# Ten more half modes of weights loaded singly, and the 64-row items moved into the middle of the output loop

## The chip, the cores and the metric

The kernel runs on one core of one Trainium2 chip. The metric is the device time of one execution in microseconds; lower is better. A core has a matrix engine (PE), three elementwise engines (DVE, ACT, POOL), a queue engine (SP), and 16 DMA engines that all queues share. DMAs are issued here from POOL (all weight loads, which also cast from float32 to float16), from SP (most stores) and from ACT.

## What is computed

Two stages, with inputs and output in float32:

```
attn = softmax(mask(q kT / 8)) v          q, k, v: 8 batches x 8 heads x 576 x 64
                                          heads 0-3: local mask; heads 4-7: strided mask
x    = attn, heads joined                 8 x 576 x 512
X    = rfft(x) over the 576 rows, first 64 modes
Y[m] = X[m] (w_r[m] + i w_i[m])           64 modes, each with two 512 x 512 matrices
u    = x + irfft(Y)
out  = u + relu(u w_ch)                   8 x 576 x 512
```

The weights w_r and w_i are 64 x 512 x 512 each, 134 MB in float32, and are read once.

## The kernel before, in words

**Order of the stages.** Attention runs first, batch by batch, while the first weights arrive. Its output is brought to the 64 modes by products with a table (`dft`). The modes are then multiplied in "half modes": the 512 input channels are split in two halves, and each pair (half, mode) has one 512 KB share of float16 weights per matrix half. `ORDER` lists all 128 half modes in the order in which they are loaded: 56 of half 1, 48 of half 0, then the last 8 of half 1 and the last 16 of half 0.

**Loading.** `w_fetch` loads two half modes at a time into one tile `wt` from the pool `pw`, which has five buffers (`NWBUF`). It is called after the second mode of a pair has been multiplied. A pair is loaded by two DMAs of 512 KB in SBUF, one from `moe_w_r` and one from `moe_w_i` (line 186), both on POOL's queue; each holds both modes of the pair. For the last four entries of `ORDER` (`i < 2 * NM - 4` is false) it uses four DMAs of 256 KB instead (line 190), in the order: first mode real, first mode imaginary, second mode real, second mode imaginary. Loads on POOL use eight completion semaphores in turn, so a load waits until the one eight before it has landed.

**The late modes.** `rest` holds the last 24 half modes. Between them PE also runs `renew`, which adds what is already known of the inverse transform to the kept rows: `v0s` (rows times `w_ch`) and `xos` (the rows themselves), and `v0h`, `xoh` for the last 64 rows of two batches. What remains after the last mode is the last quarter of the modes' spectra.

**The output loop.** After the last mode, `spec_z` and a transposition give the last spectra `zzs` (times `w_ch`) and `yys`. The output is then made in 18 items (lines 973 to 975). Each is 128 rows x 1024 columns in float32, 512 KB:

- items 0 to 7: two batches of the first four, one group of 128 rows each;
- items 8 to 15: one batch of the last four, two groups of rows;
- items 16 and 17: the last 64 rows (512 to 575) of four batches each.

Round `k` of the loop puts, on PE, the kept rows of item `k` into a PSUM pair (`v_early`), the kept rows of item `k-1` into another (`u_early`), and then the new part of both (`new_rows`, products with 32-row strips of the table `A3`, at line 1004 for the items with one batch and at 1013 for the others). ACT then takes Relu of item `k` (`v_done`), DVE adds item `k-1` into `osb` (`u_done`, line 1032), and SP stores it (line 1041). For the 64-row items, `u_done` makes four stores of 64 x 512 each (line 1044): two from SP and two from ACT. `osb` uses the five buffers of `pw`. PSUM holds three pairs "p" in turn and one pair "u": Relu parts and the even adds use "p", the odd adds "u".

**Two special places.** At `k == 6` (line 1080) a "p" pair is held for the second half of `spec_z`: four products, a copy by ACT into `zzs[1]`, and two copies by POOL into `zzs[2]` (`other`). Items of the last four batches need it. And `pieces` (line 1017) has item 0 taken in two halves by ACT, DVE and the stores, all others whole.

Of the kernel before, what the change touches and what calls it, by code (L numbers as in the profile page):

```python
# [19 lines left out]
NM = 64  # L20
# [36 lines left out]
def kernel(  # L57
# [10 lines left out]
    nc = tc.nc  # L68
# [17 lines left out]
    def psum(kind, half=False, pair=False):  # L86
        if pair:
            return pss[kind].tile([128, 2, 512], FP, tag=kind, name=kind)
        if half:
            return pss[kind].tile([128, 1024], F16, tag=kind, name=kind)  # L90
        return pss[kind].tile([128, 512], FP, tag=kind, name=kind)
# [65 lines left out]
    def w_fetch(n=1):  # L157
        for _ in range(n):
            i = len(w_tiles)
            if i >= 2 * NM:  # L160
                return
            half, m = ORDER[i]
            if i // 2 in GUEST:
                wt = big.tile([128, 2, 4, DM], F16, tag=GUEST[i // 2], name="wt")
            else:
                wt = pw.tile([128, 2, 4, DM], F16, tag="w", name="wt")
            single = []
            for ri, src in enumerate((moe_w_r, moe_w_i)):
                dst = wt[ds(64 * ri, 64)]
                rows = src[m : m + 2, ds(256 * half, 256), :].rearrange(  # L170
                    "m (p c) e -> p m (c e)", c=4
                )
                dst = dst.rearrange("p m c e -> p m (c e)")


                ones = range(2)
                if ri and not m:
                    ones = [1]
                elif i in UNEVEN and not ri:
                    a = 0  # L180
                    for n in UNEVEN[i]:
                        nc.gpsimd.dma_start(dst[a : a + n], rows[a : a + n])
                        a += n
                    continue
                elif i < 2 * NM - 4:
                    nc.gpsimd.dma_start(dst, rows)  # L186
                    continue
                single += [(j, ri, dst[:, j], rows[:, j]) for j in ones]
            for _, _, to, rows in sorted(single, key=lambda x: x[:2]):
                nc.gpsimd.dma_start(to, rows)  # L190
            w_tiles.extend((wt[:, 0], wt[:, 1]))
# [46 lines left out]
    def normalise(val, den, n, pieces, dst):  # L238
        rec = pin.tile([128, 8], FP, tag="rec", bufs=4, name="rec")
        nc.vector.reciprocal(out=rec[0:n, 0:pieces], in_=den)  # L240
        nc.vector.tensor_tensor(  # L241
            out=dst,
            in0=val.rearrange("p h (q c) -> p h c q", c=4),
            in1=rec[0:n, 0:pieces]
            .to_broadcast((n, pieces, 64))
            .rearrange("p h (q c) -> p h c q", c=4),
            op=AluOp.mult,
        )

    def act_copy(out, in_):  # L250
        nc.scalar.activation(out=out, in_=in_, func=ACTF.Copy)  # L251
# [333 lines left out]
    def mode_pair(slot, m):  # L585
        half = 1 - slot
        if m % 4 == 0:
            ypt[slot] = psum("y")
        yp = ypt[slot]
        steps = [(c, mm) for c in range(4) for mm in (m, m + 1)]  # L590
        if m == 0:
            steps.sort(key=lambda x: x[1])
        for c, mm in steps:
            wt = w_tiles[ORDER.index((half, mm))]
            pr = ds(0, 128 if mm else 64)
            a = 32 * (mm % 4)
            nc.tensor.matmul(  # L597
                yp[ds(a, 32), :],
                Xh[half][pr, c].rearrange("p b r (h m) -> p (b r h) m", h=2)[
                    :, :, mm % 32  # L600
                ],
                wt[pr, XC[c], :],
                start=(c == 0),
                stop=(c == 3),
                tile_position=(0, a),
            )
        if slot or m // 2 not in GUEST:
            w_fetch()
        if m % 4:
            yr = big.tile([128, DM], F16, tag="yr", name="yr")  # L610
            act_copy(yr, yp)
            queued.append(lambda: four_turned(slot, m - 2, yr))

    def mode(slot, m):
# [22 lines left out]
        if m % 2:  # L637
            w_fetch()
# [94 lines left out]
    def spec_z(g, bq, zp):  # L733
        for e in range(4):
            lhs = YS["YT"][:, e, g, ds(8 * bq, 8), :].rearrange("p x m -> p (x m)")
            nc.tensor.matmul(
                zp, lhs, w_chs["n"][:, e, :], start=(e == 0), stop=(e == 3)
            )
# [31 lines left out]
    strided_tokens()  # L770
    load_str(2, 2)
    w_fetch()

    def str_front(b):
# [192 lines left out]
    for n, i in enumerate([3, 5, 7] + list(range(8, 21))):  # L967
        b, t = n // 2, n % 2 * 2
# [3 lines left out]

    items = [((2 * P, 2 * P + 1), t) for t in range(4) for P in (0, 1)]
    items += [((b,), t) for b0 in (4, 6) for t in (0, 2) for b in (b0, b0 + 1)]
    items += [(range(b, b + 4), 4) for b in (0, 4)]
    LAST = len(items) - 1
    vps, ups, rls, osbs = {}, {}, {}, {}

# [6 lines left out]
    def other(spectra):  # L985
        for a in (0, 64):
            nc.gpsimd.tensor_copy(out=spectra[2][ds(64 - a, 64)], in_=spectra[1][ds(a, 64)])

    def v_early(k):
        vps[k] = psum("p", pair=True)  # L990
        for j, r in enumerate(own(items[k], v0s, v0h)):
            nc.tensor.matmul(vps[k][:, j], idn, r, start=True, stop=False)  # L992

    def u_early(k):
        ups[k] = psum(("p", "u")[k % 2], pair=True)
        for j, r in enumerate(own(items[k], xos, xoh)):
            nc.tensor.matmul(ups[k][:, j], idn, r, start=True, stop=False)

    def new_rows(k, acc, spectra):
        bs, t = items[k]  # L1000
        if len(bs) == 1:
            for j, src in ((0, spectra[1]), (1, spectra[2])):
                q = ds(32 * ((bs[0] + 2 * j) % 4), 32)
                nc.tensor.matmul(
                    acc[:, j], A3[q, out_cols(t + j)], src[q], start=False, stop=True
                )
            return
        for j, b in enumerate(bs):
            q = ds(32 * (b % 4), 32)
            o, cols = acc[:, j % 2], out_cols(t)  # L1010
            if t == 4:
                o = acc[ds(64 * (b % 2), 64), j // 2]
            nc.tensor.matmul(  # L1013
                o, A3[q, cols], spectra[b // 4][q], start=False, stop=True
            )

    def pieces(k):
        return [slice(0, 1), slice(1, 2)] if k == 0 else [slice(0, 2)]

    def v_done(k):  # L1020
        rl = ptr.tile([128, 2, 576], FP, tag=("xT", "rl")[k // 2 % 2], bufs=2, name="rl")
        rls[k] = rl[:, :, 0:DM]
        vp = vps.pop(k)
        for j in pieces(k):
            nc.scalar.activation(out=rls[k][:, j], in_=vp[:, j], func=ACTF.Relu)  # L1025

    def u_done(k):
        bs, t = items[k]
        up, rl = ups.pop(k), rls.pop(k)
        osb = pw.tile([128, 2, DM], FP, tag="w", name="osb")  # L1030
        for j in pieces(k):
            nc.vector.tensor_tensor(
                out=osb[:, j], in0=up[:, j], in1=rl[:, j], op=AluOp.add
            )
            if t < 4:
                rows = out[:, ds(128 * (t - t % 2), 256), :].rearrange(
                    "b (p i) e -> p b i e", i=2
                )
                own_b = slice(bs[0] + j.start, bs[0] + j.stop)
                to = rows[:, own_b, t % 2] if len(bs) > 1 else rows[:, bs[0], j]  # L1040
                nc.sync.dma_start(to, osb[:, j])
        if t == 4:
            for b in bs:
                (nc.scalar if b % 2 else nc.sync).dma_start(
                    out[b, ds(512, 64), :], osb[ds(64 * (b % 2), 64), b // 2 % 2, :]
                )

# [26 lines left out]
    for k in range(2):  # L1074
        if k:
            u_early(k)
        new_rows(k, ups[k], yys)
        u_done(k)
    for k in range(2, LAST + 2):
        if k == 6:  # L1080
            held = psum("p", pair=True)[:, 0]
            spec_z(3, 1, held)
            act_copy(zzs[1], held)
            other(zzs)
        if k <= LAST:
            v_early(k)
        if k > 2:
            u_early(k - 1)
        if k <= LAST:
            new_rows(k, vps[k], zzs)  # L1090
        if k > 2:
            new_rows(k - 1, ups[k - 1], yys)
        if k <= LAST:
            v_done(k)
        if k > 2:
            u_done(k - 1)
# [31 lines left out]
```

## Time and profile before

| | us |
|---|---|
| Median of 6 runs | 428.17 |
| Lowest and highest | 427.74, 429.11 |
| The profiled execution's own time | 429.11 |
| Its span in the profile | 427.3 |
| DMA busy share, average rate | 214 GB/s over the span |
| PE busy | 346.2 (81%) |
| DVE, ACT, POOL busy | 234.8, 218.2, 113.2 |
| Mean granted PE clock | 0.926 |

How to read it. The span is what the profile covers, from the first to the last instruction; the time of the execution holds a little more. Busy time of PE is modelled from pipelined matmuls, so a busy PE is not PE at its peak. The page cuts the span into 40 slices of 10.7 us and gives each engine's busy share in tenths. GB/s counts the bytes as they are written, so a float32 weight that arrives as float16 counts half. A chain of waits goes back from the last instruction to what released it, and so on; what stands in it set the end. "Landing" of a DMA is the time from its issue until all of its parts have reported.

### The profile page before, as it was taken

How to read it: one execution, taken by the hardware profiler on the slowest of the kernel's cores; microseconds unless marked ns; L12 is line 12 of the kernel's file. 1: busy time of each engine (PE TensorE's matmuls, PEld its weight loads, DVE VectorE, ACT ScalarE, POOL GpSimd, SP SyncE). 2: the span in 40 equal slices, each digit the busy share in tenths (PEclk: the TensorE clock that was granted, in tenths of full speed). 3: DMA queues.
4: the chain of work that ended last, by engine and by line, in shares of the span. 5: the costliest groups of instructions: out<-in, count | busy, mean ns of one | idle time of the engine just before them, and what ended most of it. 6: DMA issues, size and time to landing. Idle time of an engine off the chain costs nothing.

```text
span 427.3 us, 9773 instructions
## 1 busy us (share of the span) xinstructions
PE 346.2 (81%) x4167; PEld 207.4 (49%) x4167; DVE 234.8 (55%) x466; ACT 218.2 (51%) x390; POOL 113.2 (26%) x200
## 2 busy tenths in 40 slices
PE   2977878779998598789678788877879768998993
PEld 2866766654656355556433344434445323454330
DVE  3788778851446054356203247736675462564794
ACT  1687778642666356565542234422442543453772
POOL 8332333322423222222221322232232221310200
PEclk9999999957999899999985899989999985899999
DMA  8999999999999999999999999999999999995697
GB/s 152 207 212 213 212 214 212 211 211 211 214 215 212 213 212 215 214 214 213 212 214 210 212 214 215 210 212 215 212 208 214 214 213 214 214 212 100 246 372 268
DMA packets 29914, 91.62 MB, mean 214 GB/s; under 512 B 4464, under 2 KB 5232, under 8 KB 29872
## 3 DMA queue, kind: packets, MB, share of 16 engines
q0 software_dynamic: 25168, 81.28, 96.2%
q1 hardware_dynamic: 3952, 9.13, 5.7%
q8 instruction: 32, 0.52, 0.5%
q10 hardware_dynamic: 752, 0.61, 0.5%
q14 instruction: 10, 0.08, 0.0%
HBM read 162.83 MB, written 9.44 MB: 403 GB/s over the span
## 4 chain that ended last, share of the span: by engine, by line
DMA 54%; PE 24%; DVE 12%; ACT 4%; issue 2%; POOL 1%; DVEq 0%; ACTq 0%; POOLq 0%
DMA wt<-in_moe_w_i_dram 44%; DMA wt<-in_moe_w_r_dram 9%; PE y L597 5%; DVE xb L241 3%; DVE kz L283 3%; PE p L992 2%; ACT X L251 2%; PE sc L532 2%; DVE rec L240 1%; DMA ring<-in_q_dram 1%; PE tp L413 1%; PE sc L459 1%; PE y L532 1%; DVE kz L420 1%; PE av L392 1%
## 5 line engine op out<-in xcount | busy, mean ns | idle before, releaser
L597 PE MATMUL y<-wt,X 128*32 128x512 f16 (+1 forms) x448 | 69.5, 423 | 22.9 <-DMA wt<-in_moe_w_i_dram 22.9
L186 POOL DMA_DIRECT2D wt<-in_moe_w_r_dram x59 | 34.7, 588 | 115.7 <-PE y L597 24.1
L186 POOL DMA_DIRECT2D wt<-in_moe_w_i_dram x60 | 35.4, 589 | 79.0 <-DMA wt<-in_moe_w_i_dram 54.9
L597 PEld LDWEIGHTS <-X 128*32 128x32 f16 (+1 forms) x448 | 27.9, 140 | 41.1 <-DMA wt<-in_moe_w_i_dram 21.6
L727 DVE COPY xo<-tp 128x512 f16<-128x512 f16 x32 | 22.1, 691 | 36.6 <-PE tp L725 36.6
L726 ACT ACTIVATE v<-sc 128x512 f16<-128x512 f32 x32 | 19.1, 597 | 44.3 <-PE sc L717 44.3
L717 PE MATMUL sc<-w_cp,xT 128*128 128x512 f16 x128 | 36.9, 410 | 1.9 <-DVE xT L690 1.9
L241 DVE TENSOR_TENSOR xb<-av,rec 90x256 f16<-90x256 f32 (+2 forms) x80 | 36.0, 450 | 2.8
L251 ACT ACTIVATE yr<-y 128x512 f16<-128x512 f32 x28 | 16.7, 597 | 40.4 <-PE y L597 39.3
L489 ACT ACTIVATE PL<-sc 128x480 f16<-128x480 f32 (+1 forms) x48 | 26.9, 578 | 20.3 <-PE sc L475 19.9
L240 DVE RECIPROCAL rec<-av 90x4 f32<-90x4 f32 (+2 forms) x80 | 14.6, 183 | 38.6 <-PE av L504 29.2
L961 DVE TENSOR_TENSOR xo<-p,xo 128x1024 f16<-128x1024 f32 x16 | 19.6, 1224 | 21.2 <-PE p L760 21.2
L420 DVE COPY qT<-tp 128x576 f16<-128x576 f16 x16 | 11.9, 752 | 33.8 <-PE tp L413 33.8
L251 ACT ACTIVATE v<-p 128x1024 f16<-128x1024 f32 x16 | 16.4, 1024 | 20.7 <-PE p L760 20.7
L378 ACT ACTIVATE PL<-sc 90x360 f16<-90x360 f32 (+1 forms) x48 | 22.7, 490 | 6.9 <-PE sc L371 6.3
L251 ACT ACTIVATE v<-tp 128x640 f16<-128x640 f16 (+1 forms) x24 | 19.0, 807 | 11.6 <-PE tp L447 8.9
L413 PE MATMUL tp<-cI_s,ring 64*64 64x64 f16 x864 | 22.9, 198 | 2.1 <-DVE qT L420 1.7
L459 PE MATMUL sc<-cMl_s,cI_s 128*128 128x480 f16 (+1 forms) x48 | 18.7, 391 | 5.3 <-ACT PL L489 3.7
L276 PE MATMUL tp<-cI_s,ring 72*128 72x72 f16 x256 | 15.4, 207 | 8.6 <-DMA ring<-in_v_dram 7.2
L251 ACT ACTIVATE kz<-tp 64x360 f16<-64x360 f16 (+1 forms) x32 | 18.9, 592 | 6.2 <-PE tp L413 5.2
L413 PEld LDWEIGHTS <-ring 64*64 64x64 f16 x864 | 18.0, 112 | 8.3 <-issue 4.2
L1025 ACT ACTIVATE rl<-p 128x1024 f32<-128x1024 f32 (+1 forms) x19 | 18.4, 979 | 5.9 <-PE p L1013 2.0
(148 smaller groups left out, 742.0 us busy)
## 6 DMA issues: line engine op xcount, KB each, us to landing
wt<-in_moe_w_i_dram POOLq DMA_DIRECT2D x60, 512.0 KB, 18.8
wt<-in_moe_w_r_dram POOLq DMA_DIRECT2D x59, 512.0 KB, 18.0
out_dram<-osb SPq DMA_DIRECT2D x15, 512.0 KB, 2.8
ring<-in_v_dram POOLq DMA_DIRECT2D x8, 288.0 KB, 13.3
ring<-in_q_dram POOLq DMA_DIRECT2D x8, 288.0 KB, 13.6
ring<-in_k_dram POOLq DMA_DIRECT2D x8, 288.0 KB, 13.0
ring<-in_v_dram POOLq DMA_DIRECT2D x3, 512.0 KB, 14.5
ring<-in_q_dram POOLq DMA_DIRECT2D x3, 512.0 KB, 14.5
```

Of the source, the lines that this page charges most:

```text
L186: nc.gpsimd.dma_start(dst, rows)
L241: nc.vector.tensor_tensor(out=dst, in0=val.rearrange("p h (q c) -> p h c q", c=4), in1=rec[0:n, 0:pieces] .to_broadcast((n, pieces, 64)) . ...
L251: nc.scalar.activation(out=out, in_=in_, func=ACTF.Copy)
L378: nc.scalar.activation(out=PS[0:n, ds(POFF[t], 4 * n)], in_=scp[0:n, 0 : 4 * n], func=ACTF.Exp, scale=SCALE,)
L413: nc.tensor.transpose(tp[ds(64 * hp, 64), ds(64 * i, 64)], qn[ds(64 * hp, 64), ds(64 * (9 * g + i), 64)], idn[ds(64 * hp, 64), ds(64 * hp, ...
L459: nc.tensor.matmul(scp[:, 0 : n * times].rearrange("p (h x) -> p h x", h=times), idn, mask_rows("cMl", n, times), start=True, stop=False,)
L489: nc.scalar.activation(out=dst, in_=src, func=ACTF.Exp, scale=SCALE)
L597: nc.tensor.matmul(yp[ds(a, 32), :], Xh[half][pr, c].rearrange("p b r (h m) -> p (b r h) m", h=2)[:, :, mm % 32], wt[pr, XC[c], :], start= ...
L717: nc.tensor.matmul(vp, xT[:, ch], w_chs["cp"][:, ch, :], start=(ch == 0), stop=(ch == 3),)
L726: nc.scalar.activation(out=v0, in_=vp, func=ACTF.Copy)
L727: nc.vector.tensor_copy(out=xo.rearrange("p (h q c) -> p h q c", h=2, c=4), in_=tp[:, 0:512].rearrange("p (h c q) -> p h q c", h=2, c=4),)
L961: nc.vector.tensor_tensor(out=xo, in0=up[:, 0:n], in1=xo, op=AluOp.add)
```

## The change

1. `w_fetch` loads the last fourteen entries of `ORDER` singly instead of the last four: the five pairs of half modes before the last two pairs now come by twenty DMAs of 256 KB instead of ten of 512 KB. The order in which bytes are asked for changes inside each pair: first mode's real and imaginary parts, then the second mode's.
2. The two items of the last 64 rows move from the end of the list to places 8 and 13. The items of one batch are now 9 to 12 and 14 to 17.
3. The item that is last is now a whole item of 128 rows. It is taken in two halves, as item 0 is: two Relus, two adds, two stores of 256 KB.
4. Of the four stores of a 64-row item, the two that ACT issued are now issued by GpSimd (POOL).
5. The held product for `zzs[1]` moves from round 6 to round 7, since the item at place 8 doesn't read it.

```diff
@@ w_fetch
-                elif i < 2 * NM - 4:
+                elif i < 2 * NM - 14:
                     nc.gpsimd.dma_start(dst, rows)
                     continue
@@ the items
     items += [((b,), t) for b0 in (4, 6) for t in (0, 2) for b in (b0, b0 + 1)]
-    items += [(range(b, b + 4), 4) for b in (0, 4)]
+    items.insert(8, (range(0, 4), 4))
+    items.insert(13, (range(4, 8), 4))
     LAST = len(items) - 1
@@ pieces
-        return [slice(0, 1), slice(1, 2)] if k == 0 else [slice(0, 2)]
+        return [slice(0, 1), slice(1, 2)] if k in (0, LAST) else [slice(0, 2)]
@@ u_done
             for b in bs:
-                (nc.scalar if b % 2 else nc.sync).dma_start(
+                (nc.gpsimd if b % 2 else nc.sync).dma_start(
                     out[b, ds(512, 64), :], osb[ds(64 * (b % 2), 64), b // 2 % 2, :]
                 )
@@ the loop
     for k in range(2, LAST + 2):
-        if k == 6:
+        if k == 7:
             held = psum("p", pair=True)[:, 0]
             spec_z(3, 1, held)
```

On the engines' queues, PE, DVE and ACT keep their instructions in number and kind but for the halves: those of item 0's kind appear a second time at the end. POOL's queue gains ten weight loads and, behind its last copies, four stores. SP's queue has its four stores of 64 rows in the middle and two half stores at the end. ACT's queue ends with its last two Relus and no store.

## The prediction

> **What bounds the kernel now.** I read the page first (the engines' lines, the DMA line, the chain), then the chain in order of time for the last 65 us, then the timeline of the last 35 us, the stores' lines and the stretches of DMA share. From the page:
>
> ```profile
> span 427.3 us, 9773 instructions
> DMA  8999999999999999999999999999999999995697
> DMA 54%; PE 24%; DVE 12%; ACT 4%; issue 2%; POOL 1%; DVEq 0%; ACTq 0%; POOLq 0%
> ```
>
> The DMA engines are full until slice 36 (some 390 us); then comes another regime. The chain in order of time:
>
> ```profile
> 363.93 18.16 DMA wt<-in_moe_w_i_dram
> 382.09 0.28 issue
> 382.37 10.16 DMA wt<-in_moe_w_i_dram
> 392.54 0.14 issue
> 392.67 0.65 PE y L630 x16
> ...
> 401.95 1.01 ACT rl L1025
> 402.96 0.04 issue
> 403.01 0.59 PE p L992 x2
> ```
>
> The end is set by the last weights (landed at 392.54), then by a tail of 34.8 us. POOL's last weight load went out only when the load eight before it had landed (382.09): eight can be under way. In the tail the chain is PE with three visits elsewhere; one is the stall at 403.01, where PE waits for a Relu. The timeline at the tail's end:
>
> ```profile
> 417.14 0.41 PE L1013 MATMUL p<-zz,cFl_s 32*64 32x512 f16 x4
> 417.48 0.39 PE L1004 MATMUL u<-yy,cFl_s 32*128 32x512 f16 x2
> 417.80 0.60 PE L992 MATMUL p<-v0h,cI_s 128*128 128x512 f16 x2
> ...
> 420.64 1.22 DVE L1032 TENSOR_TENSOR osb<-u,rl 128x1024 f32<-128x1024 f32 x1
> 420.75 2.44 SPq L1044 DMA_DIRECT2D out_dram<-osb  x4
> 420.76 2.73 ACTq L1044 DMA_DIRECT2D out_dram<-osb  x4
> ```
>
> A normal round of the item loop starts 1.29-1.30 us after the one before (L992 at 408.39, 409.69, 410.99); the round with the first 64-row item takes 1.63 (416.17 to 417.80). DVE is done at 421.86, and 5.5 us follow in which only stores are left. Those stores, by their line:
>
> ```profile
> L1044 SPq DMA_DIRECT2D out_dram<-osb x4: 528/566/587, 420.8 to 422.6; - x4
> L1044 ACTq DMA_DIRECT2D out_dram<-osb x4: 557/583/829, 420.8 to 422.9; - x4
> DMA to landing us min/median/max: 2.4/3.1/3.5
> ```
>
> The last one is issued at 422.88 and lands 3.35 later, at 426.23; the span ends 1.1 after that. The nine full stores before them (L1041 from 408 on), 512 KB each, take one issue of 0.33 and land in 2.6 to 2.8. DMA share by stretch (after the start and end: sums, PE clock, DMA share, GB/s):
>
> ```profile
> 408.00:420.00 12.00, 12.00 (x81) 3.75 (x80) 10.79 (x10) 9.00 (x10) 0.00 (x0) 1.00 1.00 394
> 420.00:427.00 7.00, 0.27 (x4) 0.00 (x0) 1.86 (x2) 0.25 (x1) 0.00 (x0) 0.87 0.66 225
> ```
>
> PE is busy without a gap from 408 to 420 and DMA is full as well, at 406 GB/s in most single microseconds: one 512 KB item per 1.29 us. The two limits are level.
>
> [...] 64-column groups of the same mode follow each other after 0.24 us (418.77, 419.01), a group of the other mode after 0.34 (417.14 to 417.48). [...] The trace: 512 KB loads land every 2.45 us, 256 KB loads every 1.23 to 1.25. [...]
>
> **The change, part by part.**
>
> *Ten half modes loaded singly.* Ten loads of 512 KB on POOL (590 ns of issue each) become twenty of 256 KB (515 ns): POOL issues 4.4 us more, hidden, because POOL waits some 2 us before each load at this place. Bytes are the same. With eight loads of half the size under way the queue is 8 x 1.23 = 9.8 us deep; the last load already lived with that (10.16). The cost per landing: the seven landings from 382.09 to 390.7 (issue 379.92 + 10.8) are 1.236 apart, against 2.456 for a 512 KB load (POOL's releases from 370.09 to 372.52 up to 382.37, five steps), so 0.008 more per small load: 20 x 0.01 = **+0.2 us**. Does PE gain by earlier weights? The first mode of each pair could start 2.45 us sooner, but PE is at least 87% busy in every microsecond from 358 to 389 (late modes and `renew`, 358 to 367 at half clock), so it is not waiting for weights there, and it has caught up by mode 62 (weights landed 389.55, taken up at 389.65). The last two pairs were single before, and mode 63 waits for its landing in both kernels. So no gain; if in other executions PE keeps its clock, it waits earlier and not later. Bounds: 0 and +0.8 (below, B).
>
> *The zz product one round later* (k == 7). At k == 6 the held bank is followed by `v_early(6)`, which takes the bank of item 5 whose Relu ended at 402.95; PE could have gone on at 402.70 (four products of 0.215 from 401.83), and went on at 403.01: 0.31 lost. With three "p" banks in turn, at k == 7 the held one takes item 5's (free since 402.95; needed 403.12), `v_early(7)` takes item 4's second bank (DVE done 403.26; needed 403.99), `u_early(6)` item 6's first (Relu done about 404.24; needed 404.42). All free: **-0.31**. POOL's copies of zz (2 x 0.61) end about 406.2, the first item that reads them needs them at about 407.9: covered by 1.7.
>
> *64-row items to places 8 and 13.* Before, mode switches cost 0.21 (round 8, two row strips reused), 0.34 (16) and 0.23 (17): 0.78 over normal rounds. After, rounds 8, 9, 13 and 14 each mix a 64-column group with a 128-column group: 4 x 0.34 = 1.36 (the order 128 then 64, rounds 9 and 14, is not in the trace; 0.21 to 0.34, I take 0.34). Net **+0.57**; low end +0.3. So round 18 starts at 419.32 - 0.31 + 0.57 = 419.58.
>
> *The stores.* Four stores leave ACT (which queues no Relu behind them at the end, nor loses one in the middle), eight leave the end. In the middle SP issues 2 x 0.57 for such an item instead of 0.33: 1.14, within a round of 1.63. POOL issues 2 x 0.52 per item behind its zz copies; nothing is queued behind them on POOL but the second item's. The store from POOL with HBM as target is not in the trace; its landing I bound by 2.4 (SP's best for this size) and 10.2 (POOL's load behind a full queue), and take 4.8 (POOL's first load on idle engines). It must beat this: item 13's DVE work reuses item 8's buffer (five in turn). Item 8's second POOL issue starts about 410.6, DVE wants the buffer about 415.9: cover 5.3.
>
> *The new end.* Item 16's add starts 0.2 after round 18 and takes 1.23, so its store goes out at 419.58 + 1.45 = 421.03 and lands at 423.78 (2.75). The last item goes in two halves: DVE 2 x 0.68 started 0.61 apart (as item 0, from 396.53) instead of 1.22, the second half out at about 422.3. By then DMA is still moving item 16: two halves of 0.65 each (512 KB in 1.29) after 423.78 end at 425.08; on idle engines the half would land at 422.3 + 2.1 = 424.4. So 1.45 + 2.75 + 1.30 = 5.50 from round 18 to the last landing, before 426.23 - 419.32 = 6.91: **-1.41**.
>
> Sum: 0.2 - 0.31 + 0.57 - 1.41 = **-0.95**, a span of 426.4. The profiled execution took 429.11 for 427.3 of span, the slowest of the six shown; against the median 428.17 - 0.95 = 427.2.
>
> **The rivals.** (A) As summed: 427.2. Its own range is 426.8 to 427.7, since the 64-row rounds can be 0.3 cheaper and the load cost is unsure by 0.2.
> (B) The gain is eaten: the eight small loads from 382.09 to 392.54 take 1.306 each if the last, slow one (1.8) counts; were half of the excess of 0.08 the rule, twenty cost +0.8 and the sum is -0.35: 427.8. For it: the last landing. Against: the seven others.
> (C) The final stores do not queue: the half lands at 424.4, and the loads cost nothing: -0.95 - 0.7 - 0.2 = -1.85: 426.3. For it: share 1.00 need not be a ceiling. Against: landings in the two-level stretch stay at 2.8, none shorter than 2.6.
> (D) Slower: the POOL stores take the place of the tail's stores as bound, through item 8's buffer. Past a landing of 5.3 us DVE waits at item 13 and everything after it with it; past 6.3 the kernel is slower than before; at 10.2 it is 4.9 - 0.95 = +4.0: 432.1. For it: loads on that queue take 10 to 19. Against: those stand behind eight others, and here the queue is empty.
> That the change does nothing is excluded for the stores, not for the loads, where it is half of my estimate.
>
> **How the numbers follow.** 0.2% is 0.86 us, about what a measurement of this kernel can tell. A 0.52, B 0.18, C 0.22, D 0.08. Two thirds of A's range lie below 427.31: faster 0.34 + 0.22 = 0.56; same 0.18 + 0.18 = 0.36; slower 0.08. The range takes in C and B with the spread of the six times (427.74 to 429.11): 426.0 to 428.3.
>
> **What would show it.** Right: the last weight landing at 392.7; no PE gap after the held product; rounds 8, 9, 13, 14 of about 1.63; no ACT issue at the end; the last landing 1.1 to 1.4 earlier against the tail's start. Wrong: a DVE wait on a store at item 13; the last weight landing past 393.3; mode 63 not waiting for weights; or a change of PE's half-clock stretch, which would move more than any edit here.

## The result, and the profile after

| | before | after |
|---|---|---|
| Median | 427.97 us (38 runs) | 428.88 us (18 runs) |
| Lowest and highest | 427.51, 429.21 | 428.06, 430.20 |
| Profiled execution: time, span | 429.11, 427.3 | 428.9, 427.1 |
| Last weight landing to last store landing, in the profile | 392.54 to 426.23 = 33.69 | 391.57 to 425.90 = 34.33 |

After against before is 1.0019, 95% interval [1.0012, 1.0026]: slower by 0.8 us, where 427.2 (faster by 0.95) was predicted. The last weight lands between 390.9 and 392.5 in profiled executions of kernels whose loads are the same, so single profiles are compared from that landing on (last line of the table; this stretch is called the tail), and what a change is worth is taken from the times. By the table the tail is 0.64 longer; the prediction had it at 425.08 - 392.54 = 32.54.

The page of the kernel after, its span, its DMA line, the chain by engine and the full stores:

```profile
span 427.1 us, 9796 instructions
DMA  8999999999999999999999999999999999995797
DMA 52%; PE 26%; DVE 13%; ACT 4%; issue 3%; POOL 1%; DVEq 0%; ACTq 0%; POOLq 0%
out_dram<-osb SPq DMA_DIRECT2D x14, 512.0 KB, 4.1
```

At this distance little has moved, but for the last line: the median landing of a full store (a store of 512 KB) is 4.1 us after its issue, where the page of before has 2.8. This median takes in the stores of items 1 to 7, which land late in both kernels (2.9 to 4.4 here, 2.8 to 3.9 before); what the change did is seen in the single stores below. The chain in order of time (start, length, what):

```profile
381.99 9.58 DMA wt<-in_moe_w_i_dram
391.57 0.14 issue
391.71 0.65 PE y L630 x16
...
402.22 0.97 PE p L736 x4
403.19 0.43 PE p L993 x2
```

Mode 63 still waits for its weights (391.57 to 391.71), and the held product at 402.22 runs into the next round without the stall that stood at 403.01 before. The timeline of PE, one line for each start of a round (start, length):

```profile
404.31 0.61 PE L993 MATMUL p<-v0h,cI_s 128*128 128x512 f16 x2
405.94 0.61 PE L993 MATMUL p<-v,cI_s 128*128 128x512 f16 x2
407.57 0.60 PE L993 MATMUL p<-v,cI_s 128*128 128x512 f16 x2
408.87 0.60 PE L993 MATMUL p<-v,cI_s 128*128 128x512 f16 x2
```

Rounds 8 and 9 take 1.63, the next 1.30, and so again with rounds 13 and 14: as the prediction has it. The store of item 16 is issued at 420.06, 28.49 after the last weight landing; the prediction had 421.03 - 392.54 = 28.49. Up to here nothing is off. What follows is stores. Those of the full items, first behind item 8 and then behind item 13, by their line in two stretches:

```profile
L1042 SPq DMA_DIRECT2D out_dram<-osb x4: 332/341/462, 410.3 to 414.5; - x4
DMA to landing us min/median/max: 3.4/3.7/3.7
```

```profile
L1042 SPq DMA_DIRECT2D out_dram<-osb x4: 332/382/822, 417.5 to 420.7; - x4
DMA to landing us min/median/max: 4.5/4.6/4.7
```

Item 16's store lands at 424.61, 4.55 after its issue and not 2.75; the two halves of the last item follow at 425.26 and 425.90. In the kernel before, the full stores from 408 on landed in 2.6 to 2.8. And the stretches (start and end, length, PE, PE weight load, DVE, ACT and POOL busy with counts, PE clock, DMA share, GB/s), around the stores of item 8 and of item 13:

```profile
410.00:411.00 1.00, 1.00 (x8) 0.31 (x4) 0.93 (x2) 0.73 (x1) 0.35 (x1) 1.00 0.83 188
...
417.00:418.00 1.00, 1.00 (x9) 0.39 (x8) 0.93 (x2) 0.73 (x2) 0.46 (x1) 1.00 0.92 234
418.00:419.00 1.00, 0.88 (x7) 0.29 (x6) 0.93 (x2) 0.73 (x2) 0.00 (x0) 1.00 0.94 309
419.00:420.00 1.00, 0.70 (x4) 0.09 (x2) 1.00 (x2) 0.80 (x2) 0.00 (x0) 1.00 1.01 318
```

The DMA engines are busy and move little: share 0.92 at 234 GB/s, where full items move 400 to 418 at a share of 1.0. The kernel before had the same thing at its very end, and the prediction did not read it so:

```profile
422.00:423.00 1.00, 0.00 (x0) 0.00 (x0) 0.00 (x0) 0.00 (x0) 0.00 (x0) 1.00 0.97 264
423.00:424.00 1.00, 0.00 (x0) 0.00 (x0) 0.00 (x0) 0.00 (x0) 0.00 (x0) 1.00 0.95 328
```

The stores of GpSimd did what the forecast took them for (a landing of 4.8), or better: they land 2.5 and 3.2 us after their issue at item 8, 2.6 and 4.0 at item 13, and DVE does not wait for them at item 13.

### The profile page after: what moved, and what is told of

It is laid out like the page before. It is cut to its first block, busy times and chain, and to the rows that moved or that the text cites. A ratio compares the mean times of both kernels' runs of the same rounds, so it can differ in the third digit from the quotient of the medians.

```text
span 427.1 us, 9796 instructions
## 1 busy us (share of the span) xinstructions
PE 344.3 (81%) x4167; PEld 207.1 (48%) x4167; DVE 234.9 (55%) x467; ACT 218.2 (51%) x391; POOL 119.6 (28%) x214
## 4 chain that ended last, share of the span: by engine, by line
DMA 52%; PE 26%; DVE 13%; ACT 4%; issue 3%; POOL 1%; DVEq 0%; ACTq 0%; POOLq 0%
DMA wt<-in_moe_w_i_dram 39%; DMA wt<-in_moe_w_r_dram 8%; PE y L597 6%; DMA ring<-in_q_dram 5%; DVE xb L241 3%; DVE kz L283 2%; ACT X L251 2%; PE p L993 2%; PE sc L717 2%; PE sc L532 1%; PE tp L413 1%; PE y L532 1%; DVE yy L752 1%; PE sc L459 1%; DVE rec L240 1%
## 5 line engine op out<-in xcount | busy, mean ns | idle before, releaser
L597 PE MATMUL y<-wt,X 128*32 128x512 f16 (+1 forms) x448 | 68.4, 417 | 22.0 <-DMA wt<-in_moe_w_i_dram 21.6
L186 POOL DMA_DIRECT2D wt<-in_moe_w_r_dram x54 | 31.7, 587 | 111.9 <-PE y L597 41.7
L186 POOL DMA_DIRECT2D wt<-in_moe_w_i_dram x55 | 32.4, 589 | 64.7 <-DMA wt<-in_moe_w_i_dram 41.8
```

What stands on the lines that cost most here:

```text
L597: nc.tensor.matmul(yp[ds(a, 32), :], Xh[half][pr, c].rearrange("p b r (h m) -> p (b r h) m", h=2)[:, :, mm % 32], wt[pr, XC[c], :], start= ...
```

## The experiments

Three things can have cost the time: the ten more single loads, the engine that issues the 64-row stores (or the number of stores), and the stores themselves. For the last a guess of the author's, called the half theory here: a store of 64 adjacent partitions is moved at about half the rate, and two of them run side by side only if they read opposite halves. The ground for the rate is the 188 and 234 GB/s above, beside 400 to 418 for full items; for the second part the two profiles show nothing. In the middle of a stream of stores that PE fills as fast as DMA empties it (one full item per 1.30 us, at some 400 GB/s), the arrears would then never be made up.

Each text set off below says what was expected of the run under it. "Measured" is the time as a ratio to before, which was measured again beside each group of runs, with its 95% interval in brackets; microseconds are that ratio times the time of before. Where 1.0 lies inside the interval, no difference is shown.

### Loads alone, tail alone

```diff
  loads_only, against before
-                elif i < 2 * NM - 4:
+                elif i < 2 * NM - 14:
```

> The kernel before with the last fourteen half modes loaded singly, and nothing else changed. Sum theory (each of twenty small loads costs 0.01 us more than half a large one): +0.2 us over before, last weight landing at most 0.3 later. Load theory (the small loads carry the whole loss of the changed kernel): +0.8 to +0.9 us. If neither, the small loads are free: within 0.1 us.

Measured: 1.0015 [1.0007, 1.0023], so +0.6 us [0.3, 1.0].

```diff
  tail_only, against after
-                elif i < 2 * NM - 14:
+                elif i < 2 * NM - 4:
```

> The changed kernel with the loads as before (only the last four half modes singly): items, halves, GpSimd stores and the later held product alone. Tail theory (the 64-row stores in the middle move slowly, the stores behind them queue, and the end comes later): +0.6 to +0.7 us over before, full stores behind the second 64-row item landing 4.3 to 4.7 us after their issue instead of 2.75. Load theory: the tail gains what I had summed, -1.1 us.

Measured: 1.0009 [0.9999, 1.0018], so +0.4 us [0.0, 0.8]; the tail in the profile 34.02, and the full stores behind item 13 land 4.3 to 4.4 after their issue. The two parts add up to 1.0 where the whole change measured 0.8, within their intervals. The loads cost; the tail, which was to bring 1.15, brings nothing, and whether it costs is at the edge of what these times show.

### Who issues the 64-row stores

```diff
  tail_act, against tail_only
-                (nc.gpsimd if b % 2 else nc.sync).dma_start(
+                (nc.scalar if b % 2 else nc.sync).dma_start(
```

> As the tail alone, but the two stores of a 64-row item that GpSimd issued are issued by ACT again. Half theory (a store of 64 rows reads one half of the partitions, and two of them run at full rate only if they read opposite halves at the same time): SP and ACT issue opposite halves within 0.1 us of each other, so the queue behind them is shorter: 0.6 to 1.2 us below the tail alone, landings behind at 3.2 to 3.8. GpSimd theory (stores issued by GpSimd are slow by themselves): 0.5 to 1.2 us below as well. Total theory (a 64-row item costs the DMA engines the same wherever and however it is issued): same as the tail alone within 0.2 us.

Measured: 1.0037 [1.0023, 1.0050]. The timeline of this kernel behind item 8 (start, length, what, and in brackets the idle time before it with what ended it):

```profile
408.29 1.43 ACTq L1045 DMA_DIRECT2D out_dram<-osb  x2
...
409.83 1.94 ACT L1026 ACTIVATE rl<-p 128x1024 f32<-128x1024 f32 x2 [2.15 <-DVE osb L1033]
...
410.90 0.59 PE L993 MATMUL p<-v,cI_s 128*128 128x512 f16 x2 [1.38 <-ACT rl L1026]
```

ACT takes its instructions in order in this trace: it waits for DVE's add, issues two stores for 1.43, and only then comes the Relu that PE waits for, idle for 1.38. At item 13 ACT does the same (two stores in 1.39), and there DVE waits 1.26 and PE 0.63 for the Relu; PE's last product ends 2.6 later after the last weight landing than in tail_only. None of the three theories had this wait. So the move to GpSimd in the change is worth 0.28% of the time against leaving these stores with ACT: a loss avoided, and none of the loss that is to be explained.

```diff
  tail_sp, against tail_only
-                (nc.gpsimd if b % 2 else nc.sync).dma_start(
+                nc.sync.dma_start(
```

> As the tail alone, but all four stores of a 64-row item are issued by SP, one behind the other, with the halves in turn. Half theory: [...] as slow as the tail alone or up to 0.8 us slower, landings behind at 4.3 or more. GpSimd theory: no GpSimd store is left, so 0.5 to 1.2 us below the tail alone. Total theory: same as the tail alone; SP itself needs 4 x 0.57 = 2.3 us of issue in a round of 1.63, which delays the next item's store by up to 0.7 us but not the end.

Measured: 1.0001 [0.9993, 1.0009]. With all of them on SP it is 0.08% less than with half on GpSimd, and the intervals overlap, so nothing is shown for or against GpSimd. The slow stretch stays (same columns as above):

```profile
410.00:411.00 1.00, 1.00 (x9) 0.23 (x7) 1.00 (x1) 0.83 (x1) 0.00 (x0) 1.00 0.90 197
411.00:412.00 1.00, 1.00 (x12) 0.34 (x8) 0.93 (x2) 0.90 (x1) 0.00 (x0) 1.00 0.97 215
```

Two microseconds of 64-row stores, all from SP: 197 and 215 GB/s. GpSimd isn't the cause of the low rate. (In the one profiled execution the tail is 34.27, longer than before's by 0.58; the 14 times say 0.0, from -0.3 to +0.4. The times decide on the size; the profile shows where.)

### The same bytes and stores over 128 partitions

```diff
  tail_wide, against tail_sp
-                    out[b, ds(512, 64), :], osb[ds(64 * (b % 2), 64), b // 2 % 2, :]
+                    out[b, ds(512, 64), :].rearrange("p (h e) -> (p h) e", h=2),
+                    osb[:, b // 2 % 2, ds(256 * (b % 2), 256)],
```

Each store is still 128 KB, but reads 1 KB from each of 128 partitions. It writes the same 64 rows of `out` as in tail_sp, so where the bytes go is the same and only where they come from differs. The last 64 rows of the batches hold other values than they should.

> As the tail with all four stores of a 64-row item on SP, but each store of 128 KB reads 128 partitions x 1 KB instead of 64 partitions x 2 KB (the last 64 rows of the output then hold other values; bytes, number of stores and queue are the same). Half theory (engines are slow because one half of the partitions is read): over 300 GB/s instead of 200 to 215 in the microseconds of these stores, full stores behind them landing 0.8 to 1.3 us sooner than 4.2 to 4.4, the time 0.5 to 1.2 us below the version with 64 partitions. Issue theory (a store of 128 KB can't be issued faster than one per 0.6 us): the same 200 to 215 GB/s and the same time, but with a DMA share near 0.5 in those microseconds.

Measured: 0.9982 [0.9975, 0.9989], tail 33.14. Number, size and issuer of the stores are those of tail_sp, and so is PE's work (PE ends 28.13 after the last weight landing in both); 0.19% is gone. First the stores of tail_sp, then those of tail_wide (issue ns min/median/max, and landing):

```profile
L1045 SPq DMA_DIRECT2D out_dram<-osb x8: 472/588/811, 408.5 to 417.7; - x8
DMA to landing us min/median/max: 2.3/2.4/3.1
```

```profile
L1045 SPq DMA_DIRECT2D out_dram<-osb x8: 333/440/451, 409.4 to 417.9; - x8
DMA to landing us min/median/max: 1.7/1.8/1.9
```

Both issue and transfer are shorter. A microsecond of these stores, and the full stores behind item 13:

```profile
411.00:412.00 1.00, 1.00 (x8) 0.31 (x7) 0.99 (x1) 0.73 (x2) 0.00 (x0) 1.00 0.81 268
DMA to landing us min/median/max: 2.7/3.3/3.4
```

The full stores behind item 13 landed 3.1 to 4.5 after their issue in tail_sp; item 16's, issued at the same 28.49 in both, lands 1.1 earlier here. The rate of 268 misses the 300 that was expected: SP issues one such store every 0.48 us, 128 KB in 0.48 us are 273 GB/s, and the DMA engines have idle time (0.81). In tail_sp they had little (0.90 and 0.97), so there it was the transfer and not the issue that was slow.

### Fewer stores, one per half

```diff
  mid_two, against tail_only
-            for b in bs:
-                (nc.gpsimd if b % 2 else nc.sync).dma_start(
-                    out[b, ds(512, 64), :], osb[ds(64 * (b % 2), 64), b // 2 % 2, :]
+            for h in range(2):
+                (nc.gpsimd if h else nc.sync).dma_start(
+                    out[bs[0] + h : bs[0] + 4 : 2, ds(512, 64), :].rearrange(
+                        "b p e -> p b e"
+                    ),
+                    osb[ds(64 * h, 64)],
```

> As the tail alone, but a 64-row item has two stores of 256 KB, one per half of the partitions, the lower from SP and the upper from GpSimd, issued within 0.3 us of each other. Half theory: both halves are read side by side, so the item costs the DMA engines about 1.4 to 1.7 us instead of 2.3 to 2.6, landings behind it stay under 3.6, and the time is 0.6 to 1.4 us below the tail alone. Total theory (64 rows cost the same however issued): same as the tail alone.

Measured: 1.0034 [1.0022, 1.0046]. A miss: the two halves were to run side by side, and of the kernels with these items in the middle only tail_act is slower. The stretch:

```profile
409.00:410.00 1.00, 1.00 (x8) 0.31 (x7) 0.93 (x2) 0.72 (x2) 0.30 (x1) 1.00 0.31 76
410.00:411.00 1.00, 1.00 (x8) 0.31 (x7) 1.00 (x1) 0.73 (x2) 0.00 (x0) 1.00 0.97 184
411.00:412.00 1.00, 1.00 (x8) 0.31 (x6) 0.93 (x2) 1.00 (x1) 0.00 (x0) 1.00 1.06 275
```

GpSimd issues 0.27 after SP (408.42, 408.69), and with both halves asked for, 184 GB/s move from 410 to 411 at a share of 0.97, no more than in tail_sp (197 and 215). The full stores behind land 4.6 to 5.4 after their issue.

```diff
  end_two, against before (and k == 7 for k == 6)
-            for b in bs:
-                (nc.scalar if b % 2 else nc.sync).dma_start(
-                    out[b, ds(512, 64), :], osb[ds(64 * (b % 2), 64), b // 2 % 2, :]
+            for h in range(2):
+                (nc.scalar if h else nc.sync).dma_start(
+                    out[bs[0] + h : bs[0] + 4 : 2, ds(512, 64), :].rearrange(
+                        "b p e -> p b e"
+                    ),
+                    osb[ds(64 * h, 64)],
```

> The kernel before in its order (64-row items last), with their four stores each made two of 256 KB, the lower half from SP and the upper from ACT at the same time, and the held product one round later. Half theory: the last two items take 2.8 us of DMA instead of 4.4, and the last store is issued at once with the end of DVE instead of 1 us behind it: 0.8 to 1.5 us below before. If neither the halves nor the number of issues matter: 0.3 below before, from the held product alone.

Measured: 1.0014 [1.0005, 1.0022], tail 33.79. The same miss at the end of the list:

```profile
421.00:422.00 1.00, 0.00 (x0) 0.00 (x0) 0.00 (x0) 0.00 (x0) 0.00 (x0) 1.00 0.92 188
422.00:423.00 1.00, 0.00 (x0) 0.00 (x0) 0.00 (x0) 0.00 (x0) 0.00 (x0) 0.79 0.91 223
423.00:424.00 1.00, 0.00 (x0) 0.00 (x0) 0.00 (x0) 0.00 (x0) 0.00 (x0) 0.50 0.99 297
```

Two stores issued within 0.01 us of each other (419.75 by SP, 419.76 by ACT), and 188 GB/s in the first full microsecond; the four of 256 KB land 3.3 to 4.8 after their issue. The first full microsecond of both runs agrees (184 and 188); later the rate rises to 275 to 320. What is left of the half theory is the rate of 64 adjacent partitions; that two opposite halves asked for together move at the full rate from the start is refuted.

### The number 64, or that they are adjacent

Before's order of items, the 64-row items at the end, and the eight items of one batch stored as two stores of 256 KB each, all from SP. Only the choice of partitions differs, and with it which rows of `out` one store writes:

```diff
  split_half and split_even, against before
-                nc.sync.dma_start(to, osb[:, j])
+                if len(bs) > 1:
+                    nc.sync.dma_start(to, osb[:, j])
+                else:
+                    for h in range(2):
+                        part = slice(64 * h, 64 * h + 64)    # split_half
+                        part = slice(h, 128, 2)              # split_even
+                        nc.sync.dma_start(to[part], osb[part, j])
```

> The kernel before with each 512 KB store of items 8 to 15 made two stores of 256 KB from SP, of partitions 0 to 63 and 64 to 127; nothing else changed, same bytes and row lengths. Half theory: each store reads at half rate, about 210 GB/s at a DMA share near 1, so an item takes 2.5 us instead of 1.29, the buffers run out, and the time is 7 to 10 us over before. Issue theory (it is the number of stores that costs): SP's two issues of 0.55 fit a round of 1.29, so at most 1 us over before, as with the even and odd partitions.

> As the split in halves, but one store has the even partitions and the other the odd ones: 64 partitions and 256 KB each as well, in all regions of the partitions. Half theory: full rate, 390 to 410 GB/s, the time within 1 us of before. A theory of 64-partition stores as such (any 64 partitions are slow): as slow as the split in halves, 7 to 10 us over before.

Measured, two times of each: split_half 1.0122 [1.0104, 1.0140], split_even 1.0051 [1.0033, 1.0068]; 433.5 and 430.5 us, so 3.0 apart. First a stretch of split_half, then of split_even:

```profile
410.00:411.00 1.00, 1.00 (x8) 0.31 (x4) 0.93 (x2) 0.83 (x1) 0.00 (x0) 1.00 0.97 201
...
413.00:414.00 1.00, 1.00 (x9) 0.24 (x7) 1.00 (x1) 0.79 (x1) 0.00 (x0) 1.00 0.77 254
```

```profile
411.00:412.00 1.00, 1.00 (x9) 0.24 (x7) 1.00 (x1) 0.82 (x1) 0.00 (x0) 1.00 0.99 397
...
413.00:414.00 1.00, 1.00 (x9) 0.34 (x8) 0.93 (x2) 0.72 (x2) 0.00 (x0) 1.00 1.03 414
```

Sixty-four alternate partitions move at the full rate (397 to 414 GB/s), sixty-four adjacent ones at half of it for the first stores (201) and at 238 to 307 GB/s from 411 to 420. The 7 to 10 expected of split_half were reckoned with 210 throughout; at 238 to 307 the loss is smaller, and 5.2 was measured. Why the rate is higher behind the first stores was not shown. split_even lost 2.2 where under 1 was expected, and not by its rate: SP's stores come to a stop after 416.57, and the first store of the next item goes out at 421.52, right after a store of ACT has landed at 421.45 (in split_half at 424.50, after one at 424.44). By these times SP, with twice the stores, waits at this place for a store of ACT's; DMA stands empty in between (0.00 at 419 to 420). So both kernels carry that wait, and their difference is put down to the rate.

### The change with the stores spread over alternate partitions

If adjacency is the cause, the change ought to pay once the 64-row items lie across all partitions. PE can put them there in products that it makes anyway: the kept rows come in by a product with an identity, and a permuted identity is a table of the same shape (what it cost PE is read below, 28.43 against 28.49). `perm` is the identity with its columns permuted, and `A3z` has the table's 64 columns at every other place, with zeros between them.

```diff
  perm_two, against tail_only
@@ last_rows: two tables more
+        if i == 0:
+            act_copy(
+                perm.rearrange("p (r h) -> p h r", h=2),
+                idn.rearrange("p (h r) -> p h r", h=2),
+            )
+            nc.vector.memset(A3z, 0.0)
+        act_copy(
+            A3z[ds(32 * i, 32)].rearrange("p (r h) -> p h r", h=2)[:, i % 2],
+            A3[ds(32 * i, 32), 512:S],
+        )
...
@@ v_early, and u_early likewise
-            nc.tensor.matmul(vps[k][:, j], idn, r, start=True, stop=False)
+            nc.tensor.matmul(
+                vps[k][:, j], perm if items[k][1] == 4 else idn, r, start=True, stop=False
+            )
...
@@ new_rows, for t == 4
+            for j in range(2):
+                q = ds(64 * j, 64)
+                nc.tensor.matmul(
+                    acc[:, j], A3z[q], spectra[bs[0] // 4][q], start=False, stop=True
+                )
...
@@ the stores, all on SP
...
+            for h in range(2):
+                nc.sync.dma_start(
+                    out[bs[0] + h : bs[0] + 4 : 2, ds(512, 64), :].rearrange(
+                        "b p e -> p b e"
+                    ),
+                    osb[h:128:2],
```

> The tail of the changed kernel with loads as before, where the 64-row items hold one batch in the even and the other in the odd partitions (the permutation is made by the products that start the sum, and by one 64-row product instead of two 32-row ones), and where each item has two stores of 256 KB from SP, of the even and of the odd partitions. Output complete. Half theory: the item costs DMA 1.4 to 1.6 us instead of 2.4, full stores behind it land in under 3.2, and the time is 0.7 to 1.2 us below before, beating both kernels. If 64 partitions are slow wherever they lie: as the tail with all stores on SP, within 0.2 us of before.

Measured: 0.9983 [0.9972, 0.9994], median 427.55 with 428.39 for before beside it; tail 391.08 to 423.96 = 32.88. Beside tail_wide with its other values, this is the one kernel here that is faster than before and after. The stretch of item 8's stores, and the stores at the end (three full ones and the two halves):

```profile
410.00:411.00 1.00, 1.00 (x9) 0.26 (x7) 1.00 (x1) 0.77 (x1) 0.00 (x0) 1.00 1.02 377
411.00:412.00 1.00, 1.00 (x8) 0.34 (x6) 0.93 (x2) 0.96 (x1) 0.00 (x0) 1.00 1.07 420
```

```profile
L1064 SPq DMA_DIRECT2D out_dram<-osb x5: 332/338/900, 416.9 to 420.7; - x5
DMA to landing us min/median/max: 3.1/3.2/3.3
```

377 and 420 GB/s where tail_sp has 197 and 215, and landings of 3.1 to 3.3 where the kernel after has 4.5 to 4.7. Item 16's store is issued 28.43 after the last weight landing, against 28.49 for tail_sp, so PE is not what changed. Stores of 64 alternate partitions each are moved here at the rate of full items. The destination of each of these stores is that of mid_two's, where 184 GB/s were moved, so the side that is written is again not what differs.

### The two small terms

```diff
  held7, against before
-        if k == 6:
+        if k == 7:
```

> The kernel before with only the held product moved from round 6 to round 7. By my sum the stall of 0.31 us in PE goes, the items after it come 0.3 us earlier, and the time is 0.3 us below before. If the DMA engines set the end of the tail, PE's gain is lost in longer landings: no change.

Measured: 0.9995 [0.9985, 1.0004], so -0.2 us [-0.6, +0.2]. The tail in the profile is 33.37, 0.32 shorter than before's, and the stall of 0.31 is what went; the times alone can't tell that from nothing.

```diff
  loads_64, against before
-                elif i < 2 * NM - 4:
+                elif i < 2 * NM - 64:
```

> The kernel before with the last 64 half modes loaded singly instead of the last four: about 60 more loads in number, six times the ten that the change adds. If each extra load costs what the landings in the profile show (0.02 us): +1.2 us over before. If each costs what the ten seemed to cost in time (0.06 us each, 0.6 in all): +3.6. If the cost is that of a shallower queue at the end alone, paid once: +0.6 again.

Measured: 1.0046 [1.0031, 1.0060], +2.0 us [1.3, 2.6] for sixty more loads: 0.033 for each (0.022 to 0.043). Its small loads land 1.2385 apart ((392.92 - 328.52) / 52), half of a 512 KB load being 1.228, so each small landing is about 0.01 late, and a load of 512 KB turned into two is 0.02 late, at the lower end of what the times say. None of the three amounts expected lies inside the interval; 1.2, the landings' own, is nearest. For ten loads it comes to 0.2 to 0.4.

## Why the prediction was wrong

**The step that failed** is in "The new end": "its store goes out at 421.03 and lands at 423.78 (2.75)". The store goes out as predicted, 28.49 after the last weight landing, and lands 4.55 later. The two halves then follow at 0.65 each, as predicted. From that store's issue to the last landing the sum has 2.75 + 1.30 = 4.05 and the profile 425.90 - 420.06 = 5.84: 1.79 more, which is the whole gap between the predicted tail of 32.54 and the measured 34.33. The 2.75 was read from full stores with only full stores before them. The forecast put the 64-row items in the middle at their cost for SP's issues and for PE, and has no term for what they cost the DMA engines, as if their 512 KB took the 1.29 us of a full item. They are not moved at the same rate. Landing after issue of the full stores in the kernel after, in order:

| | us |
|---|---|
| ahead of item 8 | 2.85 |
| behind item 8 | 3.75, 3.69, 3.67, 3.36 |
| behind item 13 | 4.66, 4.59, 4.55 |

Each 64-row item leaves about a microsecond behind (0.90, then 1.30). PE makes 512 KB per 1.30 us and DMA empties it at that very rate, so nothing is made up but about 0.3, in one of the long rounds at item 13. In the kernel before these stores were slow too (264 to 328 GB/s), but stood last with nothing behind them. Moved ahead, they bill their time to all that follows. tail_wide against tail_sp, split_half against split_even, and perm_two show the cause: 64 adjacent partitions as the source. The number of stores (mid_two has fewer and is slower) and GpSimd (tail_sp) are excluded. What in the hardware makes adjacent partitions slow, no trace here shows.

The numbers were there. The prediction quotes 0.66 at 225 GB/s for the last seven microseconds of before and draws nothing from it; cut into single microseconds it is 0.97 at 264, busy and slow. It also says of this very spot that "the two limits are level", which means that any arrears stay.

**Ten half modes loaded singly: +0.2.** Right in kind, small in size: loads_only +0.6 [0.3, 1.0], by loads_64 0.2 to 0.4. The landings of the kernel after say what the prediction said: 28 small ones between 356.93 and 391.57, 1.237 apart against 1.228 for half a large one, which is 0.2 for twenty. What the times have over that stays open. That PE gains nothing held: mode 63 waits for its landing. Rival B's cost of 0.8 stays inside the interval of loads_only; by loads_64 it is excluded, if each load costs the same there (sixty would be +4.8). Its ground, the slow last landing of before (1.77 after the one ahead of it), does not come back in the kernel after (1.24).

**The zz product one round later: -0.31.** Right in the profile (-0.32), too small for the times.

**64-row items to places 8 and 13: +0.57.** Right: the four rounds take 1.63, the order 128 then 64 too, which the trace of before didn't have. In sum with the term before, item 16's store comes out to the hundredth.

**The stores.** ACT's relief is worth what tail_act shows, more than the text gave it: in the middle ACT would have held back a Relu. SP's 1.14 for a 64-row item is near (0.53 + 0.58). POOL's stores landed within 4.0, under the cover of 5.3 of rival D, whose wait did not come; the slower side came true by another road, a store rate that no rival named. Rival C, that the last stores don't queue, is opposite to what happened.

**The sum.** With the measured terms, against before: loads +0.2 to +0.6, held product -0.3, rounds +0.57, end -1.41 + 1.79 = +0.38. Together +0.8 to +1.2, against +0.8 measured [0.5, 1.1]. And perm_two, where the store rate is mended and the loads are left alone, has a tail of 32.88 where the prediction's own steps give 32.54: the reasoning about PE and the order of the end was nearly right for stores at the full rate. The 0.34 that is missing is in item 16's store, which still lands 3.13 after its issue and not 2.75.

## What to carry to other kernels

Read a DMA stretch by share and GB/s together: a share near 1.0 at half the usual rate is a slow transfer (0.97 at 201 GB/s in split_half, 0.99 at 397 in split_even). Where it stood decided who paid here: at the end of the stream it had nothing behind it (before), and ahead of a stream that was level with its producer it delayed the transfers behind it (landings of 3.36 to 4.66 in the kernel after, where 2.85 stood ahead). Before moving a transfer, look at which partitions it touches, not only at its bytes: 64 adjacent ones moved at half rate here at first (201 GB/s), 64 alternate ones at the full rate (397 to 414), and a permuted identity in a product that is made anyway puts rows there at no cost to PE that shows (28.43 against 28.49). And don't give ACT a store that waits for another engine while Relus are queued behind it (PE stood idle for 1.38 in tail_act).

## What the runs showed of the hardware that was not expected

- Stores of 64 adjacent partitions, in single microseconds: 184 to 223 GB/s at a DMA share of 0.90 to 0.97 (tail_sp, mid_two, end_two, split_half), and 275 to 320 at 0.88 to 1.06 later in the same stretches (mid_two, end_two); of 64 alternate partitions: 397 to 414 at 0.99 to 1.03 (split_even).
- Two stores of disjoint halves, issued within 0.3 us by two engines, moved 184 to 188 GB/s together in the first full microsecond (mid_two, end_two), where full items move 400 to 418.
- SP's issue of a store took 0.33 for 128 partitions by 4 KB (before, from 408 on), 0.47 to 0.59 for 64 partitions by 2 KB (after), and 0.47 to 1.28, in the median 0.57, for 64 partitions by 4 KB (split_half).
- Splitting a queued 512 KB load in two cost 0.03 each (0.022 to 0.043) over sixty of them (loads_64), though eight loads are under way at a time (after: the last goes out at 381.99, once the one eight before it has landed at 381.71).
